# Loading Q, K and V as bf16 by casting DMAs, with one-bank PSUM tiles in the first groups and K^T V in 64-wide tiles

## The chip, the cores and the metric

The kernel runs on one core of one Trainium2 chip. The metric is device time in microseconds (us) for one execution. A core has five engines that run side by side and wait for each other by semaphores: PE (TensorE, matrix multiplication), DVE (VectorE), ACT (ScalarE), POOL (GpSimd) and SP, which here only issues transfers. Tiles lie in SBUF, the on-chip memory; PE writes its results into PSUM, a second one, which is divided into banks. PE's clock can be throttled; the profile gives the granted share, 1.00 being full speed.

Times of one kernel vary from run to run by up to 2.3%, and most of that goes with the granted clock: 11 runs of the kernel before, made beside the first experiments, went from 323.95 us at a granted clock of 0.998 to 331.34 us at 0.969. So effects under one per cent are read from the traces below, not from the totals.

## The reference

```python
q, k, v: (8 batches, 8 heads, 576 rows, 64), float32; g_norm: (64,)
kv  = einsum('bhsd,bhse->bhde', k, v)          # K^T V, one 64x64 matrix per head
out = einsum('bhsd,bhde->bhse', q, kv)
out = out / sqrt(mean(out**2, -1) + 1e-6) * g_norm
x   = out.transpose(0, 2, 1, 3).reshape(4608, 512)
h   = x @ w_in                                  # (512, 2048)
g   = where(h > 0, h, exp(min(h, 0)) - 1)       # elu
return g @ w_out                                # (2048, 512), float32
```

The second part (the MLP) is nearly all of the arithmetic. The kernel cuts the 4608 rows into nine groups of 512. A group needs 64 large matmuls for `h` ("mm1") and 64 for the output ("mm2"). The attention of the next groups is done beside the MLP of the present one.

## The kernel before

Q, K and V are loaded as float32 into a staging tile, and an engine casts them to bf16 and rearranges them, so that the two heads `l` that share a matmul lie side by side:

```python
def fetch(name, src, b, us=None, eng=nc.sync):        # load, float32
    ...
    eng.dma_start(out=st[:, ms, :], in_=in_[:, ms, :])

def cast(name, b, u, eng, js):                        # cast and rearrange
    shape = [P, 2, RK, 2, D] if name == "q" else [P, RK, 2, 2, D]
    ...
    in_ = raw[name, b][:, u::2, js, :].rearrange("p l j d -> p j l d")
    copy_on(eng, dst, in_)
```

In the first two groups DVE, ACT and POOL share this work; from the third on POOL does all of it. K^T V is then one 64-row, 128-wide matmul per row block, of whose 128x128 result only the two 64x64 diagonal blocks are used:

```python
def kv_mm(b, kv_ps, u):
    for j in range(RK):                               # RK = 9
        for s in range(2):
            rows = slice(s * 64, s * 64 + 64)
            nc.tensor.matmul(kv_ps[:, s, u * P : u * P + P],
                lhsT=bf["k", b][rows, j, u], rhs=bf["v", b][rows, j, u], ...)
```

All of PSUM is handed out as four tiles of two banks each (A, B, S, at). Two results that share such a tile depend on each other: the second cannot be written before the reader of the first is done. Group 1's normalization puts its second mean beside a product that is still being scaled, and the output of mm2 uses the two halves of S:

```python
def ps_tile(tag, name="ps"):
    return psum.tile([P, 2, 512], FP32, name=name, tag=tag)
...
n1 = Turned(1, u, [y_mean[:, 1, :], kv_ps[:, 1, :]], [kv_ps[:, 0, :], y_mean[:, 0, :]])
...                                                    # products, then means
o_ps[T, j] = o_ps[T][:, j % 2, :]                      # mm2, o_ps[T] = ps_tile("S")
```

The elu of a pair of `h` tiles is an exp on ACT and two operations on DVE: a `tensor_scalar` (min, subtract) from SBUF to SBUF, and a `tensor_tensor` (max) that reads PSUM and writes `gT`.

## Time and profile before

| | before |
|---|---|
| median time | 327.88 us (2 runs, 327.75 to 328.01) |
| profiled execution, span | 327.8 us |
| PE busy | 291.0 us (89%) |
| POOL busy | 80.3 us (24%) |
| start of group 2's window (its first h matmul) | 102.3 us |

The windows view gives, for stretches of the span that I chose, the length, the busy time of each engine (with the number of instructions), the granted clock, the share of the DMA engines and the rate. The stretches here are: start to the last scaling of group 0, its first MLP half, its second half with attention 1, group 1's first half with attention 2, group 2's window, the windows of groups 3 to 8 without the last mm2, and the last mm2.

```profile
core 0: us, PE busy (x) PEld busy (x) DVE busy (x) ACT busy (x) POOL busy (x), PEclk, DMA share, GB/s
0.00:20.60 20.60, 16.07 (x115) 7.50 (x117) 9.92 (x19) 10.35 (x16) 9.34 (x18) 1.00 0.97 253
20.60:37.70 17.10, 12.99 (x56) 5.84 (x57) 14.55 (x14) 7.06 (x7) 6.26 (x7) 0.85 1.13 308
37.70:63.10 25.40, 19.50 (x126) 8.81 (x128) 8.39 (x15) 10.75 (x18) 6.47 (x7) 0.84 0.56 171
63.10:102.30 39.20, 29.91 (x180) 13.77 (x182) 17.29 (x23) 19.57 (x27) 12.95 (x24) 0.95 0.34 123
102.30:132.50 30.20, 26.53 (x186) 12.30 (x188) 19.45 (x22) 13.20 (x18) 11.76 (x22) 1.00 0.75 205
...
162.70:306.30 143.60, 141.86 (x860) 65.21 (x876) 85.39 (x101) 64.08 (x86) 22.00 (x43) 1.00 0.38 110
306.30:327.80 21.50, 14.34 (x64) 6.07 (x63) 3.54 (x5) 3.36 (x5) 0.00 (x0) 0.96 0.23 62
```

From 162.7 us PE is busy 141.86 of 143.60 us. In the four stretches before 102.3 us it is idle for 24 us and runs for part of the time at a reduced clock (0.85, 0.84, 0.95).

The timeline gives start, duration, engine, operation, what it writes and reads, and in brackets how long the engine was idle before and what ended the wait. This is the costliest stall of the kernel before:

```profile
29.33 1.16 POOL L94 CAST q_bf<-st_q 128x1152 bf16<-128x1152 f32 x1
29.44 3.50 DVE L332 TENSOR_SCALAR elu_e<-elu_e 128x1024 bf16<-128x1024 bf16 x1
...
30.41 1.15 POOL L94 CAST k_bf<-st_k 128x1152 bf16<-128x1152 f32 x1
31.51 1.15 POOL L94 CAST v_bf<-st_v 128x1152 bf16<-128x1152 f32 x1
33.05 1.22 DVE L335 TENSOR_TENSOR gT<-elu_e,h_ps 128x1024 bf16<-128x1024 bf16 x1
...
34.32 3.57 PE L348 MATMUL h_ps<-xT,w_in_sb 128*128 128x512 bf16 x8 [4.03 <-DVE gT L335]
```

The `tensor_scalar` at 29.44 us takes 3.50 us; its seven sisters in this stage take 0.42 to 0.73. It ends just after three POOL casts. PE waits 4.03 us for the `gT` that comes after it, and its next 8 matmuls take 3.57 us, where 8 at full clock take 1.89. (That counts to the end of the last one; from start to start, 8 take 1.73 us, the figure that the prediction uses.)

The view of the waits of PE between 42 and 60 us shows those of group 1's normalization (engine, tile and line, what it waited for: total, times, longest):

```profile
PE qt_ps L184 <- DVE xT L197: 4.4, 2, 2.2
```

### The profile page before, as it was taken

Reading aid. Unit: us, or ns where it says so; the run is one execution under the profiler, and the core shown is the slowest. Engines: PE = TensorE matmul, PEld = TensorE weight load, DVE = VectorE, ACT = ScalarE, POOL = GpSimd, SP = SyncE. Lnnn points to the kernel's source line nnn. Section 1 sums busy time; section 2 is a strip of 40 time slices with the busy share of each in tenths; the row PEclk is TensorE's granted clock in tenths of the full one; section 3 lists DMA queues with packets and bytes.
Section 4 is the critical chain, followed back from the end, with each engine's and each line's share of the span. In section 5 each row is a group of like instructions: output and inputs, shape, how many; then the busy total and the mean of one; then the engine's idle time right before and its main releaser. Section 6 shows DMA issues by size and latency. Waiting matters only on the chain.

```text
span 327.8 us, 4520 instructions
## 1 busy us (share of the span) xinstructions
PE 291.0 (89%) x1773; PEld 133.3 (41%) x1806; DVE 177.5 (54%) x220; ACT 142.2 (43%) x196; POOL 80.3 (24%) x143
## 2 busy tenths in 40 slices
PE   8786767868869986999999999999999999999984
PEld 3343333334324433444444445444444444444331
DVE  3649724162462488378547655873675476544500
ACT  3664135253673552255345435442553454333310
POOL 0836002657000364382156025500000000000000
PEclk9999597798999999999999999999999999999998
DMA  7999914768003597671695179233214042120222
GB/s 278 254 197 329 304 19 139 294 250 314 0 0 75 169 346 170 211 299 36 166 360 167 36 179 409 78 87 85 66 32 96 2 96 57 41 64 0 66 64 64
DMA packets 42068, 48.33 MB, mean 147 GB/s; under 512 B 26432, under 2 KB 30528, under 8 KB 42048
## 3 DMA queue, kind: packets, MB, share of 16 engines
q0 software_dynamic: 9984, 28.97, 27.7%
q1 hardware_dynamic: 31744, 18.55, 22.0%
q10 hardware_dynamic: 320, 0.52, 0.5%
q8 instruction: 14, 0.23, 0.3%
q14 instruction: 6, 0.05, 0.0%
HBM read 36.70 MB, written 9.44 MB: 141 GB/s over the span
## 4 chain that ended last, share of the span: by engine, by line
PE 71%; DVE 11%; ACT 9%; issue 4%; DMA 2%; another core or an unknown queue 1%; SPq 0%; ACTq 0%; DVEq 0%
PE h_ps L348 32%; PE o_ps L371 30%; DVE gT L335 5%; DVE elu_e L332 3%; ACT elu_e L325 3%; PE ps L143 3%; PE qt_ps L371 2%; ACT rT L193 2%; DMA st_v<-in_v_dram 2%; PE ps L232 1%; ACT rT L194 1%; DVE xT L197 1%; DVE xT L292 1%; ACT sq L212 1%
## 5 line engine op out<-in xcount | busy, mean ns | idle before, releaser
L348 PE MATMUL h_ps<-xT,w_in_sb 128*128 128x512 bf16 (+1 forms) x567 | 136.5, 383 | 10.2 <-DVE gT L335 7.4
L371 PE MATMUL o_ps<-w_out_sb,gT 128*128 128x512 bf16 x530 | 129.9, 386 | 7.0 <-ACT o_sb L385 2.5
L325 ACT ACTIVATE elu_e<-h_ps 128x1024 bf16<-128x1024 f32 x72 | 73.6, 1023 | 99.1 <-PE h_ps L348 95.3
L335 DVE TENSOR_TENSOR gT<-elu_e,h_ps 128x1024 bf16<-128x1024 bf16 x72 | 87.9, 1221 | 7.5
L371 PEld LDWEIGHTS <-gT 128*128 128x128 bf16 x576 | 56.1, 99 | 84.5 <-issue 17.3
L348 PEld LDWEIGHTS <-w_in_sb 128*128 128x128 bf16 x584 | 56.2, 99 | 78.8 <-issue 17.7
L332 DVE TENSOR_SCALAR elu_e<-elu_e 128x1024 bf16<-128x1024 bf16 x72 | 36.3, 504 | 92.1 <-ACT elu_e L325 92.1
L385 ACT COPY o_sb<-o_ps 128x512 f32<-128x512 f32 x30 | 17.5, 586 | 31.7 <-PE o_ps L371 28.9
L94 POOL CAST q_bf<-st_q 128x384 bf16<-128x384 f32 (+2 forms) x34 | 18.6, 589 | 30.6 <-DMA st_q<-in_q_dram 27.1
L94 POOL CAST k_bf<-st_k 128x384 bf16<-128x384 f32 (+2 forms) x34 | 18.4, 582 | 3.7 <-DMA st_k<-in_k_dram 2.8
L94 POOL CAST v_bf<-st_v 128x384 bf16<-128x384 f32 (+1 forms) x33 | 18.2, 593 | 3.0 <-DMA st_v<-in_v_dram 3.0
L263 DVE TENSOR_REDUCE ss<-sq 128x16 f32<-128x1024 bf16 x12 | 14.6, 1220 | 4.8 <-ACT sq L257 4.8
L319 POOL COPY gate<-qT 1x32 bf16<-1x32 bf16 x4 | 1.1, 272 | 62.3 <-DMA qT<-q_bf 62.3
L279 DVE TENSOR_TENSOR xs<-ps,ss 128x1024 bf16<-128x1024 f32 x12 | 14.6, 1217 | 0.0
L257 ACT ACTIVATE sq<-ps 128x1024 bf16<-128x1024 f32 x12 | 12.3, 1029 | 0.0
L84 POOL DMA_DIRECT2D st_q<-in_q_dram x8 | 5.9, 742 | 22.6 <-DVE k_bf L94 19.7
L92 ACT CAST kv_sb<-ps 128x512 bf16<-128x512 f32 (+1 forms) x8 | 4.3, 532 | 15.7 <-PE ps L143 9.3
L143 PE MATMUL ps<-v_bf,k_bf 64*128 64x128 bf16 x288 | 9.8, 217 | 0.3 <-DVE v_bf L94 0.3
L143 PEld LDWEIGHTS <-k_bf 64*128 64x128 bf16 x288 | 8.2, 94 | 3.6 <-issue 2.6
L371 PE MATMUL qt_ps<-w_out_sb,gT 128*128 128x512 bf16 x31 | 7.3, 379 | 1.6 <-ACT rT L193 1.6
L184 PE MATMUL qt_ps<-sq,ones 128*128 128x512 bf16 x6 | 2.3, 376 | 7.3 <-DVE xT L197 4.4
L197 DVE SCALAR_TENSOR_TENSOR xT<-ps,g_col,rT 128x512 bf16<-128x512 f32 x6 | 4.5, 750 | 7.4 <-ACT rT L194 7.3
(57 smaller groups left out, 118.8 us busy)
## 6 DMA issues: line engine op xcount, KB each, us to landing
st_q<-in_q_dram POOLq DMA_DIRECT2D x6, 1152.0 KB, 5.9
st_k<-in_k_dram POOLq DMA_DIRECT2D x6, 1152.0 KB, 8.5
st_v<-in_v_dram POOLq DMA_DIRECT2D x6, 1152.0 KB, 11.2
out_dram<-o_sb SPq DMA_DIRECT2D x24, 256.0 KB, 3.5
out_dram<-o_sb SPq DMA_DIRECT2D x20, 128.0 KB, 2.3
w_in_sb<-in_moe_w_in_dram POOLq DMA_DIRECT2D x4, 512.0 KB, 8.6
w_out_sb<-in_moe_w_out_dram POOLq DMA_DIRECT2D x4, 512.0 KB, 13.8
st_q<-in_q_dram SPq DMA_DIRECT2D x2, 576.0 KB, 5.4
```

Source lines behind the costliest of these rows:

```text
L94: eng.tensor_copy(out=out_, in_=in_)
L143: nc.tensor.matmul(kv_ps[:, s, u * P : u * P + P], lhsT=bf["k", b][rows, j, u], rhs=bf["v", b][rows, j, u], start=(j == 0), stop=(j == RK ...
L197: nc.vector.scalar_tensor_tensor(out=xT[T][:, cs, cols], in0=ps, scalar=g_col, in1=r, op0=ALU.mult, op1=ALU.mult)
L257: nc.scalar.activation(sq, st["se", h], AF.Square)
L263: nc.vector.reduce_sum(out=ss, in_=st.pop(("sq", h)).rearrange("p l (m e) -> p (l m) e", e=D), axis=AX.X,)
L279: nc.vector.tensor_tensor(out=st["xs"][:, 2 * h : 2 * h + 2, :].rearrange("p i (l m e) -> p l i m e", l=2, e=D), in0=se_ps.rearrange("p l ...
L325: nc.scalar.activation(e, ps, AF.Exp)
L332: nc.vector.tensor_scalar(out=e, in0=e, scalar1=1.0, scalar2=1.0, op0=ALU.min, op1=ALU.subtract)
L335: nc.vector.tensor_tensor(out=gT[T][:, 2 * i : 2 * i + 2, :], in0=e, in1=h, op=ALU.add if relu else ALU.max)
L348: nc.tensor.matmul(ps[:, a, cols], lhsT=w_in_sb[:, c, f * P : f * P + P], rhs=xT[T][:, c, cols], start=(c == 0), stop=(last and n == len(c ...
L371: nc.tensor.matmul(o_ps[T, j], lhsT=gT[T][:, f, j * P : j * P + P], rhs=w_out_sb[:, f, :], start=(f == 0), stop=(f == FC - 1),)
L385: nc.scalar.copy(o_sb[T, half][:, j % 2, :], o_ps[T, j])
```

## The change

Its intent: let the loading DMAs do the casts, so that no engine does (Q of groups 3 to 7 stays with POOL); use the data as they land, without the rearrangement; and give results that shared a two-bank tile PSUM banks of their own. Cut to its core:

```diff
-    def fetch(name, src, b, us=None, eng=nc.sync):          # float32, then cast() on an engine
+    def fetch(name, b, u=None):                             # into a bf16 tile, on POOL's queue
+        bf[name, b] = qkvp.tile([P, 4, RK, D], BF16, ...)
+        load(bf[name, b], name, b, ...)
+    def cast_q(b):                                          # Q of groups 3 to 7 only: still on POOL
 ...
-                nc.tensor.matmul(kv_ps[:, s, u * P : u * P + P],
-                    lhsT=bf["k", b][rows, j, u], rhs=bf["v", b][rows, j, u], ...)
+                for l in range(2):
+                    nc.tensor.matmul(kv_ps[s][l * 64 : l * 64 + 64, u * 64 : u * 64 + 64],
+                        lhsT=bf["k", b][rows, 2 * l + u, j, :],
+                        rhs=bf["v", b][rows, 2 * l + u, j, :], ...)
 ...
-    psum = ...tile_pool(name="psum", bufs=1, ...)           # A, B, S, at: two banks each
+    ps_m1 = ...                                             # A, B: two banks each
+    ps_m2 = ...tile_pool(name="ps_m2", bufs=2, ...)         # m: two single banks
+    ps_x = ...tile_pool(name="ps_x", bufs=2, ...)           # x: two single banks, first three groups
+    # later: ps_x is closed, "at" (two banks) takes its place; mm2's output stays in m
 ...
+    nc.vector.memset(g_col, 0.0)                            # g_norm is loaded after the first
+    nc.sync.dma_start(out=g_col[...], in_=g_src)            # K^T V, was: behind the first loads
```

In addition the transposes of Q on PE are split in two 64-wide halves, some elu pairs of group 0 get their relu from ACT, and the pieces of attention 1 and 2 are placed anew between the matmuls. Group 0's first h matmuls are no longer split into 256-wide ones, and the matmuls on zeros that only keep PE busy at the start no longer wait for the identity matrix. The 64-wide K^T V follows from the load layout: the two heads no longer lie side by side and the stationary operand "must be a [K, M] pattern with exactly one free dimension".

## The prediction

> **What bounds it now.** From 131 to 280.4 us TensorE is busy 147.6 of 149.4 us (windows view); a group takes 30.2 us, of which its 128 matmuls at 0.216 us are 27.6. The first 102.5 us hold only 224 large matmuls, 48 us at full rate: the change must earn its time there. Losses (chain, waits of PE, timeline):
> - 30.3 to 34.3 us: PE waits 4.0 us for gT: one VectorE tensor_scalar takes 3.50 us instead of 0.42 while three GpSimd casts (1.15 us each) run. Then 8 matmuls take 3.57 us instead of 1.73: half clock.
> - Group 1's normalization: two waits of 2.2 us (mean into a PSUM tile still being scaled), then slow matmuls (8 in 2.59, 12 in 4.39 us).
> - 71 to 79 us: waits of 1.6, 0.9 and 1.6 us, and 8 matmuls in 3.51 us.
> - 88 to 98 us: five waits of 0.6 to 1.5 us; 122 to 127 us: 3.4 us for gT with GpSimd casting.
>
> The Trainium skill, "TensorE: Matmul & The Clock Gate", Part 1, says an idle window of about 3.4 us halves the clock; the trace agrees (3.57 us). "GPSIMD Engine Reference", section 1, says GpSimd shares its SBUF interface with VectorE; the 3.50 us beside 3.46 us of casts agrees.
>
> **What changes.** K's and V's casts, and Q's for groups 0 to 2, leave GpSimd (55 us of casts now, some 15 left), VectorE (about 7) and ScalarE (about 3.6). DMA time should hardly change: the weights, already cast by DMA, arrive at 1 MB read in 2.5 us, like uncast Q, K, V.
>
> K^T V becomes 72 instead of 36 matmuls, half as long. Existing 64-column row-tiled ones issue every 15 ns (24 in 0.54 us), so 72 take about 1.2 us, as now (1.18). Transposes likewise.
>
> **Stage by stage** (my estimate from those durations):
> - Start to group 0's last scaling: casts go, but GpSimd issues every load (0.74 us each); V's second half lands at about 13 us. 20.6 us becomes 20 to 21.5.
> - Group 0's first MLP half without stall and slow clock: mm2 starts at about 32, not 37.7. Gain 5.5.
> - mm2 of group 0 with attention 1, means in banks of their own: ends at about 55, against 65.7 for the same work. Gain so far 10.
> - Group 1's MLP with attention 2: new waits, above all K^T V of the second half, whose bank frees late (3.5 us), and two of 1 us at the products. The group 2 window starts at about 89.5, not 102.5.
> - Group 2's window: 1 us gained. Then same within 0.5 us a group.
>
> Sum: about 13 us gained, all critical: **315.0 us, range 308 to 321.5**. Chances: faster by over 2% 0.87, within 2% 0.11, slower 0.02.
>
> **Checks in the profile.** VectorE's longest tensor_scalar in 20 to 40 us under 1 us; mm2 starts at 31 to 33 us; no granted clock below 0.9 between 20 and 60 us; GpSimd busy under 40 us; a group's K^T V 1.1 to 1.5 us; group 2's window at 86 to 93 us; period later 30.2 us; one wait over 2 us of K^T V at about 70 us.
>
> **What would make it wrong.** Casting loads slower than assumed, or GpSimd's waits for earlier loads delaying weights or group 1's K and V; 64-wide matmuls not overlapping; new waits at 70 to 85 us cooling the clock; or fewer waits than I count, which gives below 310.

## The result, and the profile after

| | before | after |
|---|---|---|
| median time | 327.88 us (2 runs) | 309.31 us (2 runs, 309.03 to 309.59) |
| ratio, 95% interval | | 0.943 (0.939 to 0.947) |
| the same again, 6 runs beside 11 of before | 327.61 us | 308.77 us, ratio 0.948 (0.943 to 0.953) |
| POOL busy | 80.3 us | 46.4 us |
| start of group 2's window | 102.3 us | 86.7 us |

Ratios here and below are the mean time of one kernel's fast runs over that of the other's of the same rounds, so not quite the ratio of the medians. Runs that the measurement marked as slow (three of the eleven of the first batch) are left out of the ratios. The outputs of all kernels in this text agree with the reference.

The same stretches in the windows view of the changed kernel (columns as before):

```profile
0.00:22.90 22.90, 16.98 (x160) 7.05 (x161) 5.46 (x15) 8.75 (x14) 12.36 (x22) 0.93 1.04 165
22.90:34.20 11.30, 11.29 (x52) 5.07 (x52) 8.98 (x14) 9.01 (x15) 4.35 (x6) 1.00 1.23 206
34.20:53.90 19.70, 18.55 (x197) 8.69 (x196) 7.65 (x15) 9.04 (x19) 5.11 (x7) 1.00 1.20 235
53.90:86.70 32.80, 27.49 (x225) 12.35 (x224) 17.35 (x25) 18.68 (x31) 3.02 (x6) 0.95 0.31 74
86.70:115.60 28.90, 26.41 (x225) 11.97 (x225) 18.86 (x22) 12.41 (x17) 5.41 (x10) 1.00 0.74 173
...
145.30:288.10 142.80, 141.59 (x985) 64.28 (x984) 85.12 (x101) 63.49 (x86) 10.62 (x19) 1.00 0.41 94
288.10:306.90 18.80, 14.06 (x65) 6.06 (x63) 3.54 (x4) 3.36 (x5) 0.00 (x0) 0.94 0.26 70
```

The profiled executions differ by 20.9 us of span. By stretch (before minus after; 12 of the mm2 matmuls, 2.6 us, moved from the fourth stretch into the third):

| stretch | before | after | gained |
|---|---|---|---|
| start to last scaling of group 0 | 20.6 | 22.9 | -2.3 |
| first MLP half of group 0 | 17.1 | 11.3 | 5.8 |
| its second half, attention 1 | 25.4 | 19.7 | 5.7 (8.3 for the same work) |
| group 1's first half, attention 2 | 39.2 | 32.8 | 6.4 (3.8 for the same work) |
| group 2's window | 30.2 | 28.9 | 1.3 |
| groups 3 to 8 without the last mm2 | 173.8 | 172.5 | 1.3 |
| the last mm2 | 21.5 | 18.8 | 2.7 |

Two to four of the 20.9 us are luck of the draw: the profiled execution of the kernel before took 329.6 us at a clock of 0.971. The eight fast runs of the kernel before in the first batch below have a mean of 326.6 us at a clock of 0.988, the six of the changed kernel 309.3 us at 0.986. So over these runs the change did not raise the granted clock, but the trace of the kernel before has 17.1 us at half clock between 32.6 and 77.0 us, where that of the changed kernel has 6.8 us before 76 us. That makes the gains of the second to fourth stretch look larger than they are in a usual run.

What answers to the stall at 29 us. In the tile view (operation, count: duration in ns, least, median and most, and when), the `tensor_scalar` of this stage of the changed kernel:

```profile
L359 DVE TENSOR_SCALAR elu_e<-elu_e x8: 418/419/528, 24.6 to 35.2; 128x1024 bf16<-128x1024 bf16 x8
```

None is over 528 ns now, and in the windows view PE is busy 11.29 of the 11.30 us of this stage at clock 1.00.

The start has become longer. The chain of the work that ended last (start, duration, what) runs from 10 to 23 us through the small load of g_norm:

```profile
10.66 6.29 DMA g_col<-in_g_norm_dram
16.95 0.03 issue
...
17.08 0.76 DVE xT L213
...
17.97 1.01 PE h_ps L379 x2
```

The load is two transfers of 256 bytes, issued at 10.01 us and just after; the data are there only at about 17 us, and the scaling and the next matmuls wait for it. And the new wait in attention 2 that the prediction named is there (timeline of the changed kernel):

```profile
69.08 0.22 PE L157 MATMUL kv_ps<-v_bf,k_bf 64*64 64x64 bf16 x2 [1.41 <-issue]
...
71.35 0.47 PE L157 MATMUL kv_ps<-v_bf,k_bf 64*64 64x64 bf16 x34 [2.06 <-DVE xT L213]
...
71.75 2.99 PE L379 MATMUL h_ps<-xT,w_in_sb 128*128 128x512 bf16 x8
...
74.68 1.17 PE L175 MATMUL qt_ps<-ident,q_bf 128*64 128x128 bf16 x18
```

K^T V starts at 69.08 us after an idle time of 1.41 us, stops after two matmuls until the second scaling frees its bank (2.06 us), and the 8 matmuls after it take 2.99 us instead of 1.89: the clock has dropped. The windows view of this stretch (71 to 76 us) has 0.66.

How much such a wait costs is in part luck. In every trace here the clock is full or half, and it changes only at steps of 3.41 us, whose position differs from run to run. The windows view of two such steps in the changed kernel, and below of two in a run with nearly the same waits here (1.12 and 2.06 us; it is the run with the two-bank output tile, further down):

```profile
69.00:72.41 3.41, 1.28 (x39) 0.80 (x40) 2.19 (x3) 1.22 (x4) 0.00 (x0) 1.00 0.00 0
72.41:75.82 3.41, 3.41 (x25) 1.57 (x24) 0.00 (x0) 1.02 (x1) 0.00 (x0) 0.50 0.00 0
...
69.34:72.75 3.41, 1.59 (x40) 0.96 (x41) 1.76 (x2) 0.83 (x3) 0.00 (x0) 1.00 0.00 0
72.75:76.16 3.41, 3.29 (x33) 1.47 (x32) 1.50 (x2) 1.23 (x2) 0.00 (x0) 1.00 0.00 0
```

PE is busy for 1.28 us of the step in one run and the next step has half clock; in the other it is busy for 1.59 us and the clock stays full.

K^T V of one group in the later windows, first a line of the timeline of the kernel before:

```profile
166.20 1.18 PE L143 MATMUL ps<-v_bf,k_bf 64*128 64x128 bf16 x36
```

And the same piece of work in the timeline of the changed kernel:

```profile
119.12 0.78 PE L157 MATMUL at<-v_bf,k_bf 64*64 64x64 bf16 x72
```

Twice as many matmuls take 0.78 us instead of 1.18. The period of the later windows falls from 30.1 us (first h matmul at 132.53, then 162.65) to 29.7 (115.57, then 145.29); the one after that takes 30.2, so the mean gain is smaller than this pair shows.

The last mm2, in the timeline of the kernel before (only PE's lines of matmuls):

```profile
306.35 3.67 PE L371 MATMUL o_ps<-w_out_sb,gT 128*128 128x512 bf16 x16
...
310.74 3.40 PE L371 MATMUL o_ps<-w_out_sb,gT 128*128 128x512 bf16 x15 [0.72 <-ACT o_sb L395]
...
315.03 3.61 PE L371 MATMUL o_ps<-w_out_sb,gT 128*128 128x512 bf16 x16 [0.89 <-ACT o_sb L395]
...
319.31 3.61 PE L371 MATMUL o_ps<-w_out_sb,gT 128*128 128x512 bf16 x16 [0.67 <-ACT o_sb L395]
```

And in the timeline of the changed kernel:

```profile
288.13 14.03 PE L400 MATMUL o_ps<-w_out_sb,gT 128*128 128x512 bf16 x64
```

Before, each block of 16 matmuls waits for ACT's copy of the block before it, which sits in the other half of the same two-bank tile. After, the 64 run without a pause: 14.03 us instead of 16.57.

### The profile page after: what moved, and what is told of

The parts are those of the page before. It is cut to its first block, busy times and chain, and to the rows that moved or that the text cites. A ratio compares the mean times of both kernels' runs of the same rounds, so it can differ in the third digit from the quotient of the medians.

```text
span 306.9 us, 5144 instructions
## 1 busy us (share of the span) xinstructions
PE 285.8 (93%) x2136; PEld 128.9 (42%) x2136; DVE 165.6 (54%) x217; ACT 138.3 (45%) x204; POOL 46.4 (15%) x81
## 4 chain that ended last, share of the span: by engine, by line
PE 77%; DVE 9%; ACT 5%; DMA 4%; issue 3%; POOL 0%; SPq 0%; DVEq 0%; POOLq 0%
PE h_ps L379 36%; PE o_ps L400 36%; DVE gT L363 5%; ACT elu_e L351 3%; DMA v_bf<-in_v_dram 2%; DMA g_col<-in_g_norm_dram 2%; DVE elu_e L359 2%; PE at L251 1%; DVE xT L213 1%; PE at L157 1%; ACT rT L209 1%; ACT rT L210 1%; DVE xT L313 1%; PE kv_ps L157 1%; PE mean L200 1%
## 5 line engine op out<-in xcount | busy, mean ns | idle before, releaser
L379 PE MATMUL h_ps<-xT,w_in_sb 128*128 128x512 bf16 x576 | 136.6, 384 | 6.5 <-DVE xT L213 3.0
L351 ACT ACTIVATE elu_e<-h_ps 128x1024 bf16<-128x1024 f32 (+1 forms) x77 | 73.9, 972 | 85.7 <-PE h_ps L379 82.4
L363 DVE TENSOR_TENSOR gT<-elu_e,h_ps 128x1024 bf16<-128x1024 bf16 (+1 forms) x73 | 85.6, 1177 | 8.1 <-PE h_ps L379 0.5
L416 ACT COPY o_sb<-o_ps 128x512 f32<-128x512 f32 x32 | 18.5, 588 | 34.2 <-PE o_ps L400 34.2
L213 DVE SCALAR_TENSOR_TENSOR xT<-y_ps,g_col,rT 128x512 bf16<-128x512 f32 x12 | 8.9, 748 | 17.7 <-ACT rT L210 15.3
L104 POOL CAST q_bf<-st_q 128x384 bf16<-128x384 f32 x30 | 14.7, 534 | 24.6 <-DMA st_q<-in_q_dram 20.0
L300 DVE TENSOR_TENSOR xs<-at,ss 128x1024 bf16<-128x1024 f32 x12 | 14.6, 1217 | 0.0
L278 ACT ACTIVATE sq<-at 128x1024 bf16<-128x1024 f32 x12 | 12.3, 1028 | 0.0
L209 ACT ACTIVATE rT<-mean,eps_col 128x512 f32<-128x512 f32 x12 | 8.2, 682 | 6.1 <-PE mean L200 5.9
L482 PE MATMUL idle_ps<-zeros 128*128 128x512 bf16 x30 | 8.8, 437 | 1.2 <-DVE eps_col L473 1.2
L89 POOL DMA_DIRECT2D v_bf<-in_v_dram x11 | 8.2, 745 | 5.4 <-DMA w_in_sb<-in_moe_w_in_dram 1.8
```

The lines of the kernel that those rows point to most:

```text
L89: nc.gpsimd.dma_start(out=dst.rearrange("p m j d -> p m (j d)")[:, ms, :], in_=in_[:, ms, :])
L104: nc.gpsimd.tensor_copy(out=bf["q", b][:, u, js], in_=raw[b][:, u::2, js, :].rearrange("p l j d -> p j l d"),)
L278: nc.scalar.activation(sq, st["se", h], AF.Square)
L300: nc.vector.tensor_tensor(out=st["xs"][:, 2 * h : 2 * h + 2, :].rearrange("p i (l m e) -> p l i m e", l=2, e=D), in0=se_ps.rearrange("p l ...
L351: nc.scalar.activation(e[:, lo:hi, :], h, AF.Exp)
L363: nc.vector.tensor_tensor(out=gT[T][:, 2 * i + lo : 2 * i + hi, :], in0=e[:, lo:hi, :], in1=h, op=ALU.add if relu else ALU.max,)
```

## The experiments

Twelve runs in three batches, each with 6 timed executions beside 11 of the kernel before on the same chip. The first is the changed kernel itself, as a reference. It and the three others of its batch ran on one chip, the later two batches on another, so a comparison of two ratios across batches carries both intervals (about 0.5% each way).

> The changed kernel unaltered, once more, as the reference for the other runs: 309 us (308.5 to 310), 0.943 of the kernel before.

Measured: 308.77 us median (307.98 to 311.03), ratio 0.948. As expected at the median; the spread is wider than I wrote.

### Is the stall at 29 us POOL's doing?

My theory was that POOL's casts hold up DVE's `tensor_scalar`, and that PE then waits and cools. The rival was a shortage of PSUM tiles. In the kernel before, I gave only those three casts to DVE and ACT:

```diff
-    for name in "qkv":
-        cast(name, 1, 0, Q, all_js)
 ...
-        if u == 1:
-            cast("q", 1, 1, V, low); cast("q", 1, 1, A, high); ...   # k, v likewise
+        for name in "qkv":
+            cast(name, 1, u, V, low)
+            cast(name, 1, u, A, high)
```

> The kernel before, with only one thing altered: the three GpSimd casts of group 1's first half (1.15 us each, at 29 to 33 us) are done by VectorE and ScalarE instead, as those of the second half are. Theory (GpSimd's casts hold up VectorE's tensor_scalar, which holds up PE, which cools its clock): the longest tensor_scalar between 20 and 40 us falls from 3.50 to under 0.8 us, the 4.0 us wait of PE and the 8 slow matmuls (3.57 us) go, mm2 starts at 32 to 34 us instead of 37.7; the kernel takes 321 to 325 us. Rival (the stall is a shortage of PSUM tiles, whatever GpSimd does): the wait of about 4 us stays and the time is 327 to 329 us.

Measured: 324.36 us median, ratio 0.993 (0.988 to 0.999). In the tile view the `tensor_scalar` of the stage are now all alike:

```profile
L332 DVE TENSOR_SCALAR elu_e<-elu_e x8: 419/420/428, 22.6 to 34.2; 128x1024 bf16<-128x1024 bf16 x8
```

PE's wait for `gT` shrinks from 4.0 to 0.5 us, its matmuls keep the full clock in this stage, and mm2 starts at 32.76 us instead of 37.69. The theory stands and the rival falls. But of the 4.9 us gained there, 2.2 (by the ratio) to 3.3 us (by the medians) remain at the end. In part the casts now stand in DVE's and ACT's way: PE waits 1.2 us for the cast of Q right after. In part the 4.9 us are the draw of the trace. The run with only K^T V altered (below) leaves this stage as it was, and its trace is a second sample of the stall: the `tensor_scalar` takes 3.38 us, but PE waits 0.5 and 2.7 us instead of 4.0, and mm2 starts at 35.43 us. Against that, 2.7 us were gained.

The other way round, I put three useless casts of the same size on POOL in the changed kernel:

```diff
     for s in (2, 3):
         load_w_out(s)
+    for _ in range(3):
+        nc.gpsimd.tensor_copy(out=junk_bf, in_=junk)     # 128x1152, float32 to bf16
```

> The changed kernel with three useless GpSimd casts of the old size put back (fp32 to bf16, 128x1152) at about 30 us, between the loads. Theory: one tensor_scalar of VectorE takes 2 to 3.5 us, PE waits 2 to 4 us before or in the first mm2 matmuls, possibly with slow matmuls after it; 312 to 316 us. Rival (the one-bank tiles and the relu on ScalarE had removed the stall by themselves): VectorE is held up, but PE does not wait over 1 us and the time stays at 309 to 310.5 us.

Measured: 310.38 us median, ratio 0.953. Neither expectation was right: the time lies in the rival's range, the wait in neither. The two `tensor_scalar` that met the casts took 1.32 and 1.25 us, not 2 to 3.5, and PE waited 1.9 us. All three casts write the same tile here, so a semaphore wait stands between them (0.06 us from the end of one to the start of the next), which in the kernel before did not. So I gave each its own tile:

> As the run with three useless GpSimd casts put back, but each cast writes its own tile, so that no wait stands between them (as in the kernel before). In the earlier run the two tensor_scalar that met them took 1.32 and 1.25 us, one cast each. Theory (VectorE gets in only where GpSimd pauses between two casts): one tensor_scalar of 2.3 to 3.6 us, PE waits 2.5 to 4.5 us at the first mm2, 310.5 to 313 us. Rival (each tensor_scalar is held by one cast at most, and the 3.50 us of the kernel before came from the interleaved layout of its casts): none above 1.4 us, time as in the earlier run, 309.5 to 311.5.

Measured: 313.50 us median, ratio 0.959 (0.954 to 0.963), that is 1.1% over the changed kernel's 0.948. In the timeline:

```profile
29.36 0.74 POOL L125 DMA_DIRECT2D w_out_sb<-in_moe_w_out_dram  x1 [0.67 <-DMA q_bf<-in_q_dram]
29.75 3.96 DVE L361 TENSOR_SCALAR elu_e<-elu_e 128x1024 bf16<-128x1024 bf16 x1
...
30.09 3.33 POOL L475 CAST junk_bf<-junk 128x1152 bf16<-128x1152 f32 x3
...
34.55 1.89 PE L381 MATMUL h_ps<-xT,w_in_sb 128*128 128x512 bf16 x8 [1.30 <-DVE gT L365]
...
38.52 2.75 PE L402 MATMUL o_ps<-w_out_sb,gT 128*128 128x512 bf16 x12 [2.08 <-DVE gT L365]
```

The `tensor_scalar` takes 3.96 us. It starts while POOL is still issuing a load (29.36 to 30.10 us) and ends 0.29 us after the last cast. PE waits 1.30 and 2.08 us. So a run of POOL operations without a pause keeps DVE out for its whole length, and with a pause after each cast for one cast only. The stall of the kernel before is reproduced by its suspected cause. The time of 313.5 lies a little above the range that I wrote for this theory.

The Trainium skill, "SBUF — State Buffer", "Who interferes with whom", says that a DVE operation in a two-port mode and a POOL operation exclude each other for the length of a whole instruction. The 1.32 us beside one cast agree; that a row of POOL instructions is not broken up is what the 3.96 us add.

### K^T V in 64-wide tiles alone

```diff
+                for l in range(2):
+                    nc.tensor.matmul(kv_ps[l * 64 : l * 64 + 64, s, u * 64 : u * 64 + 64],
+                        lhsT=bf["k", b][rows, j, u, l], rhs=bf["v", b][rows, j, u, l], ...)
```

(in the kernel before, with its own layout; `kv_sb` shrinks accordingly)

> The kernel before with only K^T V altered to 64-wide tiles on four quarters of the array (its own layout of K and V kept). Theory (the tiles overlap fourfold): a group's K^T V takes 0.78 instead of 1.18 us on PE, and since PE bounds the later groups, 2 to 3.5 us are saved: 324.5 to 326 us. Rival (issue of instructions bounds it: twice as many take as long): 1.1 to 1.3 us and 327.5 to 328.5 us.

Measured: 327.57 us median, ratio 1.002 (0.997 to 1.007): the total shows no gain. The trace shows the time that the theory gives: 72 matmuls in 0.78 us instead of 36 in 1.18, and a period of 29.9 us (161.83 to 191.69) instead of 30.1. (That it is an overlap of four tiles is inferred from this time.) In the profiled execution PE waits 5.0 us for `gT` in group 2's window, against 3.4 in the kernel before, and the six runs have a mean granted clock of 0.976 against 0.988 for the eight fast runs of the kernel before. So the rival about the issue of instructions falls. That the waits elsewhere took back the 2 us is likely, but one trace doesn't show it for all runs.

### The two-bank output tile alone

In the changed kernel, mm2's output from group 2's window on is again two halves of one tile:

```diff
-            o_ps[T, j] = single("m", "o_ps")
+            if j % 2 == 0:
+                o_ps[T] = ps_s.tile([P, 2, 512], FP32, name="o_ps", tag="S")
+            o_ps[T, j] = o_ps[T][:, j % 2, :]
```

> The changed kernel with one part undone: from group 2's window on, the two output tiles of mm2 in flight are again the halves of one two-bank tile, as before. Theory (the last group's mm2 then waits for the copy out of the neighbouring bank, as in the kernel before, where the 64 last matmuls took 16.6 us instead of 14.0): PE waits three times 0.6 to 0.9 us in the last 15 us, the last 64 matmuls take 16 to 17 us, all windows before that unchanged; 2 to 3 us slower than the changed kernel at the same granted clock. Rival (the waits at the end came from something else, such as late stores): the last 64 matmuls stay at 14.0 us.

Measured: 310.90 us median, ratio 0.953 (0.947 to 0.958). The totals alone leave it open. The trace doesn't: PE's waits for ACT's copy at the end are back.

```profile
PE o_ps L402 <- ACT o_sb L427: 2.1, 3, 0.7
```

The last 64 matmuls run from 286.86 to 303.43 us, 16.6 us as in the kernel before, and PE's other waits from 90 us on are those of the changed kernel.

### A bank for each mean

In the changed kernel, group 1's second mean goes into the pool of the products, where it must wait for the first scaling, as before:

```diff
-            n.sums(l, single("m", "mean"))
+            n.sums(l, single("mx"[l], "mean"))
```

> The changed kernel with one part undone: in group 1's normalization the second mean gets no bank of its own but that of the first product, so it waits for the first scaling, as in the kernel before. Theory: two waits of about 2.2 us of PE at the second mean in 36 to 60 us, the K^T V of the second half waits longer, and the clock may drop after them: 3.5 to 7 us slower than the changed kernel. Rival (the PE queue has enough to do, the waits only move): under 2 us slower.

Measured: 315.02 us median, ratio 0.964, 1.7% over the changed kernel, about 5.2 of its 308.8 us. Timeline of this run:

```profile
43.26 0.58 PE L200 MATMUL mean<-sq,ones 128*128 128x512 bf16 x1 [2.22 <-DVE xT L213]
...
43.64 3.26 PE L400 MATMUL o_ps<-w_out_sb,gT 128*128 128x512 bf16 x8
```

The wait of 2.22 us is exactly that of the kernel before, and the 8 matmuls after it take 3.26 us instead of 1.89. The same happens again at 52.7 us, where the 24 matmuls that follow take 7.03 us instead of 5.34. Group 1's mm1 starts at 59.79 us instead of 53.93. Of this some 3.4 us are waits (4.4 less the 1.0 that K^T V no longer waits) and some 3 are the clock. The theory stands.

### The wait for g_norm

```diff
+    g_src = ...
+    for l in range(2):
+        nc.sync.dma_start(out=g_col[...], in_=g_src)     # first of all
     for u in range(2):
         for name in "qkv":
             fetch(name, 0, u)
 ...
-    nc.vector.memset(g_col, 0.0)                          # and the load at this place
```

> The changed kernel with g_norm's small load issued first of all on its own queue instead of at 10 us. In the profile of the changed kernel the first scaling waits for this load until 17.1 us (issued at 10.0) and PE 2.9 us for the scaling. Theory (this wait is critical): g_col is there before 10 us, the scaling of the first half starts at about 15.5 us, the last scaling of group 0 starts at 19.3 to 20.5 us instead of 22.1, and 1.5 to 3 us are saved at the same granted clock. Rival (the chain through the second half bounds the start, and the small load delays the first Q by as much): under 0.7 us saved.

Measured: 307.05 us median, ratio 0.940, 0.8% below the changed kernel's. The scaling starts at 14.62 us, and the last one at 20.14 instead of 22.11:

```profile
14.62 1.40 DVE L213 SCALAR_TENSOR_TENSOR xT<-y_ps,g_col,rT 128x512 bf16<-128x512 f32 x2
...
16.24 0.77 PE L379 MATMUL h_ps<-xT,w_in_sb 128*128 128x512 bf16 x2 [1.08 <-DMA w_in_sb<-in_moe_w_in_dram]
...
20.14 0.75 DVE L213 SCALAR_TENSOR_TENSOR xT<-y_ps,g_col,rT 128x512 bf16<-128x512 f32 x1 [0.53 <-ACT rT L210]
```

The next wait behind it, for the first part of w_in, is 1.1 us here (2.1 us in the trace of the version that combines this with the next change). The load was critical.

### The wait of K^T V in attention 2

```diff
-        5: lambda: (late_norm(0, 1), late_kv(1)),
-        6: lambda: late_q(1),
+        5: lambda: late_norm(0, 1),
+        6: lambda: (late_kv(1), late_q(1)),
```

> The changed kernel with K^T V of group 2's second half moved one MLP step later (after the seventh pair of h tiles instead of after the sixth), so that the bank it takes over from the first product is free by then. In the changed kernel PE waits 1.4 and 2.1 us there, and the next 8 matmuls take 2.99 us instead of 1.73 and 18 transposes 1.17 instead of 0.69. Theory (the wait and the cold clock after it are critical): both waits go, those 8 matmuls take under 2 us, group 2's window starts 3.5 to 5.5 us earlier; 303.5 to 305.5 us. Rival (the wait comes back a step later, at the products): under 2 us saved.

Measured: 305.02 us median, ratio 0.939. That is 0.9% below the changed kernel's ratio. Of the waits of 1.4 and 2.1 us one of 0.95 is left, and the matmuls after it keep the full clock (timeline of this run):

```profile
70.86 0.47 PE L157 MATMUL kv_ps<-v_bf,k_bf 64*64 64x64 bf16 x34 [0.95 <-DVE xT L213]
...
71.89 1.90 PE L379 MATMUL h_ps<-xT,w_in_sb 128*128 128x512 bf16 x7
```

The rival is right in a small part: PE's waits for `gT` between 60 and 125 us grow to 3.9 us, from 2.8 in the changed kernel.

### A version that beats both

> The early load of g_norm (2.0 us saved alone) and the later K^T V together. The two stages follow one another, so the savings should add: 301.5 to 303.5 us. If the first only moves a later wait, under 3.5 us are saved in all.

Measured: 303.26 us median (302.21 to 304.63), ratio 0.932 (0.927 to 0.936) to the kernel before. This is the fastest of all that ran, 1.7% under the changed kernel by the ratios, and the two savings add within the noise.

Then two attempts to go on. For the first, mm2's leftover halves in group 2's window move to later h steps:

```diff
-        second = {i: (...) for i in range(8 - lead)}
+        first = 2 if T == 2 else 0
+        second = {i + first: (...) for i in range(8 - lead)}
```

> As the last, and in group 2's window the four half tiles of mm2 left over are placed after h steps 2 to 5 instead of 0 to 3, where VectorE has the sums and scalings as well. In the changed kernel PE waits 2.5 us for gT at the last two h steps of this window. If VectorE bounds those steps, this wait falls below 0.8 us and 1.5 to 2.5 us more are saved: 299.5 to 301.5 us. Otherwise a wait appears at the products of group 3, and the time stays within 1 us.

Measured: 305.91 us median, ratio 0.939: slower. PE's waits for `gT` fell to 0.7 us as hoped, but the products of group 3 now come too early for the DMA transpose of their Q:

```profile
88.35 0.28 PE L251 MATMUL at<-kv_sb,qT 64*64 64x64 bf16 x11 [2.82 <-DMA qT<-q_bf]
...
88.56 2.70 PE L379 MATMUL h_ps<-xT,w_in_sb 128*128 128x512 bf16 x8
```

It seems that the removed matmuls had covered that transfer; the new wait of 2.82 us cools the clock as well (8 matmuls in 2.70 us). The last run adds a shift of four mm2 matmuls ahead of group 1's second K^T V:

```diff
-        mm2_all(*((6, 8), (10, 15))[u])
+        mm2_all(*((6, 9), (11, 15))[u])      # the other two ranges move along
```

> As the last, and in group 1's attention four matmuls of mm2 are moved in front of the second half's K^T V, which waits 1.0 us for its bank in the changed kernel. The wait should fall to about 0.1 us and the time by 0.5 to 1 us, hardly to be told by the total: 299 to 301 us.

Measured: 305.01 us median, ratio 0.937. The wait at that K^T V falls from 1.0 to 0.4 us, and the total is not told apart from the run before. The range that I wrote for both runs was missed because of the transpose.

## Why the prediction was right or wrong

The direction, the size and the place were right: 315.0 us (308 to 321.5) forecast, 309.31 measured. The gain was 18.6 us instead of 13. The terms of the sum:

- **"Start ... becomes 20 to 21.5"**: wrong, 22.9. Not the loads of Q, K and V but the load of g_norm, which the change moved to 10 us, was last. Issued first, it gives back 2.0 us. I had the line of the diff in view and costed only the large loads.
- **"Group 0's first MLP half without stall and slow clock ... Gain 5.5"**: right, 5.8 for this stretch. Because of the late start mm2 begins at 34.2, not at 31 to 33 us, so that check failed. The runs with POOL's casts taken away and put back show the cause as forecast. The check on the clock failed in one place: after the wait for g_norm it is 0.67 on average from 18.0 to 22.9 us (half until 21.2 us).
- **"mm2 of group 0 with attention 1 ... ends at about 55"**: 53.9, although it began 2.2 us late. For the same work 8.3 us were gained, where the forecast had about 4.5 (10 less the 5.5 before it); this is the term that was mis-sized most. The banks for the means are worth 5.2 us here, as the run that undid them shows.
- **"Group 1's MLP with attention 2 ... The group 2 window starts at about 89.5"**: 86.7. The new wait was found where forecast, 3.5 us in two pieces, with a cold clock after it; two waits at the products are 0.9 us in all instead of 2. Even with those, the stretch is 3.8 us shorter for the same work. Which of the changes there brought that (fewer POOL casts, more banks) was not taken apart.
- **"Group 2's window: 1 us gained"**: 1.3.
- **"Then same within 0.5 us a group"**: right for the windows (1.3 us in six groups), but nothing was forecast for the last mm2, and in all 4.0 us were gained after group 2's window (173.8 and 21.5 against 172.5 and 18.8). K^T V was estimated at 1.2 us from the 15 ns between 64-wide matmuls that use two parts of the array; on four parts it takes 0.78. And the last mm2 is 2.5 us faster, which I had not looked at: I took the one-bank tiles for a matter of the first three groups, but mm2's output uses them to the end.

So the late start (2.3 us lost) hid part of a gain that was larger than forecast in every other stretch. That the total came out inside the range is in part luck, since these errors offset each other; the prediction had named "fewer waits than I count, which gives below 310". By the ratios, POOL's casts put back cost 3.6 us, the shared bank for the means 5.2 and the two-bank output 1.6, together some 10 of the 17 to 19 us; the rest was not taken apart. POOL came to 46 us, not under 40: its casts take 14.7 us as counted, but its 41 loads, at 0.72 to 0.77 us each, take 30 more.

## What to carry to other kernels

A row of small casts on POOL can cost several microseconds on PE when it falls beside DVE's SBUF-to-SBUF work: look for one operation of DVE that is many times longer than its sisters. Two results that share a PSUM tile share their waits, so look for PE waiting on the reader of the neighbour, at the end of the kernel too. After removing waits, follow the chain of the changed kernel again from its start: here a load of 512 bytes and one misplaced piece of attention were worth another 1.7%, and a step that filled a gap elsewhere took the cover from a transfer.

## What the Trainium skill lacked or had wrong

- "TensorE: Matmul & The Clock Gate": Part 1 ("Wait — 56ns, not 53.3ns?") gives about 25 ns as the least distance from one matmul's start to the next, however small; Part 3 has about 4 ns between the tiles of one pack. Here a stream of 72 matmuls of 64x64 on four quarters of the array, each with its own weight load, starts at 90.27 us in the changed kernel and the next large matmul at 90.97: under 10 ns apart. The floor of Part 1 doesn't hold for tiles, and neither part has a figure for such a stream.
- "TensorE: Matmul & The Clock Gate", Part 1: it asks for an idle window of about 3.4 us for the half clock, and has no busy share at which the clock drops. Here the window need not be idle. The clock records of the 14 traces change at steps of 3.41 us: after all 42 steps in which PE was busy for less than 43% the clock was half, and above that after only two (47 and 52%, both at 13 us beside small matmuls) of some 1170. So waits of 2.22 us (8 matmuls in 3.26 us after it) and 2.82 us (2.70 us) could be enough, and waits of 1.89 and 2.08 us (12 matmuls in 2.75 us after each, in the two runs with casts put back) were not. The half rate itself agrees: 3.57 us for 8 matmuls.
- "SBUF — State Buffer", "Who interferes with whom": it doesn't say that a row of POOL instructions is not broken up for a waiting DVE operation. One `tensor_scalar` took 3.96 us beside three casts without a pause, and 1.32 us where a semaphore wait stood between them.
- "DMA: Bandwidth & Descriptors" says that a cast makes a transfer a GpSimd-issued one, but gives no rate for it. Here casting loads moved 206 GB/s counted where written as bf16, which is 412 GB/s as read, from 23 to 46 us of the changed kernel.
- The same page gives no time for a tiny load beside large ones. Here the second of two 256-byte transfers on a queue of their own took 6.3 us while large loads were in flight on another.
